# Sketched attention and a token-mixing block on one core: wider quads for batches 2 and 3, a shorter last chunk, and another written-down order

## The chip, the core and the metric

The kernel runs on one core of a Trainium2 chip. The core has five engines that each work through an instruction list of their own: TensorE (PE, whose weight loads are listed as PEld), VectorE (DVE), ScalarE (ACT), GpSimd (POOL) and SyncE (SP, which only issues DMAs here). The metric is device microseconds of one execution, as a median of several runs.

## The reference

Attention with a sketched kernel comes first (4 batches, 4 heads, 1088 tokens, head width 32; S1 and S2 are 8 x 32), and then a token-mixing block on its output x, which has 128 channels per token (4 heads of 32):

```python
phi(t) = outer(S1 @ t, S2 @ t)            # 64 features of a token and head
kv  = einsum('bhsf,bhsd->bhfd', phi(k), v)
den = einsum('bhsf,bhf->bhs', phi(q), phi(k).sum(s)) + 1e-6
x   = einsum('bhsf,bhfd->bhsd', phi(q), kv) / den      # then (b, s, h*d)
theta  = x @ w_theta
zr, zi = x * cos(theta), x * sin(theta)
y   = w_tok_r @ zr + w_tok_i @ zi         # w_tok: 1088 x 1088, over tokens
u   = x + y
out = u + relu(u @ w_ch)
```

q, k and v are float32. S1, S2 and the weights of the block come as 64-bit words and are brought to float32 in the kernel.

## The kernel before

**Data and tiles.** A batch's 1088 tokens stand as nine chunks of 128 (the last has 64 that count). Three chunks make a group, so there are three groups per batch. x is kept turned, channels on partitions, in a tile xT of 1152 columns. The two w_tok matrices come as 17 double rows of 1088 KB (row0 to row16), each loaded into a zs buffer (L642), unpacked by two ACT activations (L643, L645) and two DVE operations (L647 to L649), and kept in big buffers. The input loads of 576 KB are at L655 to L671, those of the second halves of k's chains at L714 with an accumulating DMA that POOL issues (L393). q of batch 3 arrives in 16 small DMAs (L663), since it is loaded already turned in blocks.

**Stages of a batch.** key_sums (L677), kfeatures (L767, features of k and the products with v, stage kv), chain and chain_out (L835, L933, which scale these sums), query_scale and query_slices (L985, L1007), levels (L1033: features of q as a product with weights of 128 tokens and a denominator, then lv on ACT, L1056), outputs_x (L1088: numerators, stage num), theta and z (L1169 to L1227: the products with w_theta, sine and cosine on ACT, z on DVE), and the mixing. Batches 0 and 1 are mixed by mix_row (L1256): 17 double rows of w_tok against z, summed in PSUM, and mix_out. Batches 2 and 3 are mixed together in winograd (L1352): seven block products m1 to m7 (stages named m) in place of eight, on sums of blocks of w_tok. Two of the four sums, "ac3" and "ac4" (L379, names APOOL at L153), are 16 adds of 128x544 on POOL; the other two, ac1 and ac2, are 16 such adds on DVE; zc1 to zc4 are sums of z on DVE. finish (L1282) and finish_turned (L1329, the last 160 tokens) compute u + relu(u @ w_ch) and store it.

**Numerators of batches 2 and 3.** For each group, DVE makes the features qp (L1100), turns blocks of 32 x 32 of them into qt (L1109), and TensorE runs 32 products with 32x32 weight tiles (heads of kv in bd) on 96 columns each (L1112 to L1117, the quads). Four ACT copies per group (L1121) put the results into xT. So there are three quads operations of 32 products per batch.

**Order and buffers.** Nothing is scheduled at run time. Every operation is recorded with an engine letter (P, V, A, G or S), the buffers that it reads and writes, and a number. ORDER (L34) is the sequence in which the operations are issued, written out by hand or by a planner beforehand: 1020 numbers. Each engine gets its own operations in that order. STARTS (L80) holds a planned start for each, from which two things follow. In run (L248) an operation's buffers take the free slot of their class that has been free longest. In issue (L267) padding is put before TensorE's operations between two marks (first at L431, last at L1470), `int((o.start - last - 0.08) * FILL)` products of 384 columns on an idle tile (L427, L428). This makes 28 padding products. Buffer classes (L344) are fixed numbers of slots: big 22, zs 5 of 2176 floats, g3 5 of 768 floats, g1 6, ps 8 banks of PSUM, and others. An operation whose slot still belongs to another buffer waits for that buffer's last reader.

Input loads in SP's order, before: k3, q0, row1, k2, w2, q2, row3, h1 (a second part of k of batch 1, added to the first by POOL's DMA), v0, row8, q1, row2, v1, row0, v3, h3, row7, row5, row4, h2, half of q3, row6, v2, row9, the other half of q3, row10, 13, 11, 15, 14, 12, 16. k0 and k1 are issued by ACT.

## Time and profile before

| | |
|---|---|
| time, median of 3 runs | 217.79 us (217.53 to 218.53) |
| the profiled execution: span | 215.9 us, granted clock 0.995 |
| the profiled execution: span and what lies around it | about 217.8 us |
| TensorE busy | 208.9 us, 2396 records |
| DVE, ACT, POOL busy | 174.3, 114.5, 59.7 us |
| quads (32x32 tiles, 96 columns) | 384 records |
| padding products of 384 columns | 28 |
| POOL adds 128x544 | 16, mean 1458 ns |
| first and last 10 us: TensorE busy | 7.7 us of 0 to 10; 22.0 of the last 26 |

How to read it: the page gives the busy time of each engine and its share of the span, then the span in 40 slices of 5.4 us with a digit of busy tenths per engine, the granted clock and the DMA rate; then the chain of waits that ended last; then groups of instructions (line, engine, operation, output and inputs by name, shape, count, busy time and mean of one, idle time before and what ended it). Busy time of pipelined products overlaps, so a product's mean is longer than the distance from one start to the next. A float32 product leaves two records.

### The profile page before, as it was taken

What the parts mean: (1) busy time and instruction counts of PE and PEld (TensorE: products, weight loads), DVE (VectorE), ACT (ScalarE), POOL (GpSimd) and SP (SyncE); (2) the same over time, 40 slices, a digit from 0 to 9 for tenths busy, and PEclk for the clock granted to TensorE, in tenths of its full rate; (3) what the DMA queues carried; (4) which work ended last, traced back from release to release, by engine and by line L of the source; (5) the groups of instructions that cost most, each with busy time, mean ns of one, the idle gap of its engine ahead of it and who ended that gap; (6) DMA issues with size and microseconds to landing.
All of it is one profiled execution on the core that took longest, in us unless ns stands there. A gap on an engine that the chain in (4) does not pass through costs nothing.

```text
span 215.9 us, 5832 instructions
## 1 busy us (share of the span) xinstructions
PE 208.9 (97%) x2396; PEld 152.8 (71%) x2396; DVE 174.3 (81%) x343; ACT 114.5 (53%) x256; POOL 59.7 (28%) x105
## 2 busy tenths in 40 slices
PE   7899999999999999999999999999999999999992
PEld 7677798868866666866668666667677776666781
DVE  1799998999999998999999798885994747456263
ACT  4899989999998895798704233363810000000000
POOL 1272740306400000604004100000006489950403
PEclk9999999999999999999999999999999999999998
DMA  6999999995998993192002402424050420010735
GB/s 222 395 418 419 384 365 420 425 315 97 360 285 267 416 432 145 75 308 45 0 0 32 74 3 112 114 109 112 2 88 15 67 39 0 0 23 8 125 55 103
DMA packets 28046, 37.09 MB, mean 172 GB/s; under 512 B 20564, under 2 KB 23044, under 8 KB 25844
## 3 DMA queue, kind: packets, MB, share of 16 engines
q1 hardware_dynamic: 22868, 31.86, 42.4%
q0 software_dynamic: 1552, 3.25, 7.2%
q10 hardware_dynamic: 3600, 1.62, 2.8%
q8 instruction: 19, 0.31, 0.6%
q14 instruction: 7, 0.06, 0.1%
HBM read 29.84 MB, written 4.00 MB: 157 GB/s over the span
## 4 chain that ended last, share of the span: by engine, by line
PE 63%; DMA 18%; ACT 14%; issue 2%; SPq 1%; DVE 1%; POOL 1%; POOLq 0%; ACTq 0%
PE ps L399 61%; DMA zs<-w_tok 13%; DMA big<-k_l 5%; ACT big L645 4%; ACT big L643 3%; ACT lv L1056 1%; PE ps L1131 1%; ACT big L1021 1%; ACT g L1199 1%; ACT g L1202 1%; ACT g L1205 1%; ACT g L1203 1%; POOL out L1299 1%; SPq L671 0%; ACT g L1135 0%
## 5 line engine op out<-in xcount | busy, mean ns | idle before, releaser
L399 PE MATMUL ps<-big,zs 128*128 128x384 f32 (+2 forms) x380 | 110.5, 436 | 0.0
L399 PEld LDWEIGHTS ps<-big,zs 128*128 128x128 f32 x380 | 66.9, 190 | 32.5
L379 POOL TENSOR_TENSOR big<-big,big 128x544 f32<-128x544 f32 x16 | 22.1, 1458 | 48.6 <-DVE big L379 44.6
L399 PE MATMUL ps<-big,big 128*32 128x32 f32 (+2 forms) x352 | 22.8, 234 | 0.0
L643 ACT ACTIVATE big<-zs 128x1088 f32<-128x1088 f32 x17 | 20.9, 1231 | 1.5 <-DMA zs<-w_tok 0.9
L379 DVE CUSTOM_DVE_ANT_0 big<-big,big 128x2176 uint16<-128x2176 uint16 x17 | 21.5, 1275 | 0.0
L645 ACT ACTIVATE big<-zs 128x1088 int32<-128x1088 uint32 (+1 forms) x18 | 21.4, 1194 | 0.3 <-DMA zs<-w_tok 0.3
L1338 ACT COPY big<-ps 80x256 f32<-80x256 f32 x1 | 0.4, 368 | 39.6 <-DMA out<-g 39.6
L399 PEld LDWEIGHTS ps<-big,big 128*32 128x32 f32 (+1 forms) x352 | 15.3, 124 | 6.8 <-issue 0.8
L1276 ACT COPY g<-ps 128x384 f32<-128x384 f32 (+1 forms) x6 | 2.5, 466 | 23.4 <-PE ps L399 23.4
L379 DVE TENSOR_TENSOR big<-big 128x544 f32<-128x544 f32 x8 | 9.5, 1204 | 5.6 <-PE ps L399 5.6
L383 DVE TENSOR_SCALAR big<-big 128x1088 int32<-128x1088 int32 x17 | 12.2, 719 | 0.0
L379 POOL TENSOR_TENSOR mf<-mv,sm 128x32 f32<-128x32 f16 (+1 forms) x3 | 0.8, 262 | 39.1 <-DVE sm L379 39.1
L428 PE MATMUL ps<-idle 128*128 128x112 bf16 (+1 forms) x67 | 10.0, 312 | 1.3 <-POOL idle L430 1.3
L379 DVE TENSOR_TENSOR g<-lv 128x768 f32<-128x768 f32 x12 | 11.1, 950 | 0.1
L399 PEld LDWEIGHTS ps<-w,big 128*128 128x128 f32 (+1 forms) x76 | 9.8, 189 | 1.4
L379 DVE TENSOR_TENSOR big<-big,hf 128x1152 f32<-128x1152 f32 x8 | 10.7, 1351 | 0.0
L399 PE MATMUL ps<-w,big 128*128 128x128 f32 (+1 forms) x76 | 10.5, 278 | 0.0
L399 PE MATMUL ps<-sbk,g 128*128 128x64 f32 x72 | 10.0, 276 | 0.3 <-ACT g L793 0.3
L379 DVE TENSOR_TENSOR zs<-zs,g 128x384 f32<-128x384 f32 (+2 forms) x24 | 9.8, 447 | 0.2
L386 DVE SCALAR_TENSOR_TENSOR big<-ps,even,big 128x384 f32<-128x384 f32 (+1 forms) x10 | 4.8, 493 | 6.3 <-PE ps L399 6.2
L1199 ACT ACTIVATE g<-ps 128x384 f32<-128x384 f32 x12 | 5.9, 504 | 7.3 <-PE ps L399 7.3
(199 smaller groups left out, 379.2 us busy)
## 6 DMA issues: line engine op xcount, KB each, us to landing
zs<-w_tok SPq DMA_DIRECT2D x17, 1088.0 KB, 10.6
big<-k_l SPq DMA_DIRECT2D x5, 576.0 KB, 13.2
big<-v_l SPq DMA_DIRECT2D x4, 576.0 KB, 15.6
big<-q_l SPq DMA_DIRECT2D x3, 576.0 KB, 10.7
big<-hf POOLq DMA_DIRECT2D x3, 576.0 KB, 10.0
far<-zs SPq DMA_DIRECT2D x3, 576.0 KB, 2.8
zs<-far SPq DMA_DIRECT2D x12, 144.0 KB, 4.3
big<-k_l ACTq DMA_DIRECT2D x2, 576.0 KB, 4.4
```

Of the source, the lines that this page charges most:

```text
L379: eng.tensor_tensor(out=o, in0=a, in1=b, op=f)
L383: (eng or V).tensor_scalar(out=o, in0=a, scalar1=s1, scalar2=s2, op0=op0, **kw)
L386: (eng or V).scalar_tensor_tensor(out=o, in0=a, scalar=s, in1=b, op0=op0, op1=op1)
L399: T.matmul(o, lhs, rhs, start=start, stop=stop, skip_group_check=True)
L428: T.matmul(nowhere()[:, :n], idle()[:, 0:P], idle()[:, :n], start=True, stop=True, skip_group_check=True)
L643: op("A", 0.22 + n * 0.0009, lambda: A.activation(dfn(), words_of(raw(), n)[1].bitcast(F32), AF.Prelu, scale=2.0**-112, alpha=-(2.0**32)), ...
L645: op("A", 0.22 + n * 0.0009, lambda: A.activation(stp(), words_of(raw(), n)[0].bitcast(U32), AF.Copy, scale=2.0**-29), [stp], [raw])
L1021: op("A", act(GW) + 0.1, lambda g=g, tr=tr: A.activation(f()[:, g * GW:(g + 1) * GW], tr(), AF.Copy, scale=s()[:, 0:1]), [(f, g)], [tr, (s ...
L1056: op("A", act(480), lambda g=g, lp=lp: A.copy(lv().rearrange("p l (c n) -> p l c n", n=HR)[:, :, g * GC:(g + 1) * GC], lp().rearrange("p c ...
L1131: T.transpose(tr()[:, i * P:(i + 1) * P], qp()[:, i * H + 2 * n:i * H + 2 * n + 2].rearrange("p h i j -> p (h i j)"), ident())
L1199: op("A", act(GW), lambda cs=cs, th=th: A.activation(cs()[:, 0], th(), AF.Copy, bias=ROUND), [(cs, 0)], [th])
L1276: op("A", act(w), lambda: A.copy(u(), yp()[:, :w]), [uT], [yp])
```

## The change

- **Quads.** The turned features of all three groups of a batch go into one buffer qt of class zs, and the 32 products of a batch are issued once, on 288 columns. Four copies of 288 columns replace twelve of 96. The DVE transposes stay three per batch.
- **Levels.** The ninth chunk uses 64 tokens as weights instead of 128 and writes 64 output rows.
- **finish_turned.** The transposes, the ACT copy and the products become operations of their own. The result is computed in a buffer of its own, yb, in place of xT, and an empty operation goes.
- **Classes.** zs becomes 2304 floats wide, g3 has 4 slots.
- **The order.** ORDER has 1001 numbers, and is another one. STARTS and the slot search go: slots are listed in SLOTS (391 buffers), and padding in GAPS, five products in three places.

What moves, in the order: kv2 to the first half (behind 45 us of TensorE's own work, before 69); kv3 to behind about 82 us; the rows of batch 0's mixing begin only after the first theta product of batch 1, and run mixed with those of batch 1; the sums of w_tok that POOL makes stand all behind ac2_0, while ac1_6, ac2_2 to ac2_7, zc3 and zc4 stand behind on DVE. SP's load order after is h1, k2, q0, k3, v0, h3, q1, h2, row1, q2, v1, w2, row0, row8, row3, half of q3, row6, row4, row5, v2, the rest of q3, row2, v3, the batch 1 round trip, row9, 7, 11, 10, 14, 13, 15, 12, 16.

The diff, cut to its core (ORDER, STARTS and SLOTS are lists of numbers):

```diff
 ORDER = (
...
-STARTS = (
...
+GAPS = {11: 1, 110: 3, 177: 1}
+SLOTS = (
...
 WARM = 0
-FILL = 5.0
...
-TILE16, TILE32, TILE64, QUAD = 0.045, 0.12, 0.15, 0.65
+TILE16, TILE32, TILE64, QUAD = 0.045, 0.12, 0.15, 1.25
...
+        for b, slot in zip([b for b in self.bufs if b.cls is not None], SLOTS):
+            b.slot = slot
+
+    def issue(self, pools, fill):
         for o in self.order:
...
+            for _ in range(GAPS.get(o.i, 0)):
+                fill()
...
-        "zs": (5, 2176),
+        "zs": (5, 2304),
...
-        "g3": (5, 768),
+        "g3": (4, 768),
...
-                    x = f()[:, (g * GC + i) * P:(g * GC + i + 1) * P]
-                    mm(o(i)[:, 2 * HR:], x, mf[b]().rearrange("p t h r -> p (t h r)"), False, i == GC - 1)
+                    c = g * GC + i
+                    n = min(P, S - c * P)
+                    x = f()[:, c * P:c * P + n]
+                    mm(o(i)[:n, 2 * HR:], x, mf[b]().rearrange("p t h r -> p (t h r)"), False, i == GC - 1)
...
+        qt = buf("zs", (NC, H, 2, SQ), F32, "qt") if b in QUADS else None
...
-                qt = buf("g3", (GC, H, 2, SQ), F32, "qt")
-                xq = [buf("ps", (GC, SQ), F32, "xq") for _ in range(NQ)]
...
+                vop(CH * R * R, lambda g=g, qp=qp: V.transpose(
+                    out=qt()[:, g * GC:(g + 1) * GC].rearrange("p c h f t -> p (c h f t)"),
+                    in_=qp().rearrange("p n i j -> p (n i j)")), [(qt, g)], [qp])
                 continue
...
+        if b in QUADS:
+            at("num", b)
+            xq = [buf("ps", (NC, SQ), F32, "xq") for _ in range(NQ)]
+
+            def quads():
+                for f in range(2):
+                    for j in range(NQ):
+                        for h in range(H):
+                            u = slice(j * SQ, (j + 1) * SQ)
+                            mm(xq[j]()[h * D:(h + 1) * D], bd()[u, f, h], qt()[u, :, h, f], f == 0, f == 1)
+
+            op("P", QUAD, quads, xq, [bd, qt], hold=[xt])
...
-            A.copy(y(), pu()[:n, 0:2 * DM])
...
+        op("P", 0.2, turned, [pu], keys, hold=[yb])
+        op("A", act(2 * DM), lambda: A.copy(y(), pu()[:n, 0:2 * DM]), [yb], [pu])
+        op("P", 0.35, products, [po], keys + [w2])
```

## The prediction

> **What bounds the kernel now.** I read the busy times first, then the slices, then the chain that ended last, then the groups and the waits of TensorE, and the timeline where DVE and POOL meet. The page's busy times:

> ```profile
> PE 208.9 (97%) x2396; PEld 152.8 (71%) x2396; DVE 174.3 (81%) x343; ACT 114.5 (53%) x256; POOL 59.7 (28%) x105
> ```

> TensorE is busy in all but 7 us. Its slices and the DMA's tell that there are two stages:

> ```profile
> PE   7899999999999999999999999999999999999992
> ...
> ACT  4899989999998895798704233363810000000000
> POOL 1272740306400000604004100000006489950403
> ...
> GB/s 222 395 418 419 384 365 420 425 315 97 360 285 267 416 432 145 75 308 45 0 0 32 74 3 112 114 109 112 2 88 15 67 39 0 0 23 8 125 55 103
> ```

> A slice is 5.4 us. Up to about 48 us the loads move some 400 GB/s, ACT and DVE are full, and TensorE's busy time there is partly padding. From 50 us to the end TensorE runs product after product. The chain of waits agrees:

> ```profile
> PE 63%; DMA 18%; ACT 14%; issue 2%; SPq 1%; DVE 1%; POOL 1%; POOLq 0%; ACTq 0%
> PE ps L399 61%; DMA zs<-w_tok 13%; DMA big<-k_l 5%; ACT big L645 4%; ACT big L643 3%; ACT lv L1056 1%; PE ps L1131 1%; ACT big L1021 1%; ACT g L1199 1%; ACT g L1202 1%; ACT g L1205 1%; ACT g L1203 1%; POOL out L1299 1%; SPq L671 0%; ACT g L1135 0%
> ```

> In order of time this chain is loads of k and w_tok to 31.6 us, ACT unpacking until 66, one load until 77, and TensorE from 78.4 to 210.4. So a product less after 50 us is time saved, while before 46 us what counts is when loads and unpacked rows arrive. From starts of consecutive records I get pitches (a 384-column f32 product, two records, 2 x 323 ns; a record of 128 or 96 columns about 110 ns). Adding these up in written order, TensorE's work ends at 202.65 us; its last product ends at 212.05. The difference, 9.4 us, I call the lag. It is already about 10 us at 46 us: TensorE loses time only early, and it does so to these:

> ```profile
> L399 PE MATMUL ps<-g,g 32*32 32x96 f32 x384 | 5.8, 252 | 0.0
> L428 PE MATMUL ps<-idle 128*128 128x384 bf16 x28 | 6.2, 327 | 0.0
> ```

> The first row is the quads (the numerators of batches 2 and 3), the second the 28 padding products, which stand in written order and cost their pitch of 0.163 us each, 4.6 us in all, whether the wait they were meant to fill is there or not.

> The profiled execution took its span, 215.9 us, and about 1.9 us around it, 217.8, which is the median of 217.79; terms are taken from that.

> **The quads.** Six groups of 64 records each, 384 in the row. In one group the first record starts at 119.08 us and the next 128x128 product at 119.98: 0.89 us, of which 0.72 is 64 starts and 0.17 the way back. All six: 5.34 us. After, each batch has one set: 64 records of 288 columns over 16 tiles, four per tile. A 384-column record takes 323 ns, so one of 288 takes 0.242 and four 0.97; with 0.17 behind and about 0.1 to get going, 1.25 us, an estimate. Two batches 2.50; saved 2.84. Bounds: if nothing is paid to get going, 1.13 each (saved 3.1); if starts scale with columns, 3 x 0.72 + 0.17 = 2.33 each (saved 0.7). I take 2.8, since 11 ns per record before is far under a 96-column pass (81 ns over 16 tiles is 5), so the records were bound by their starting, not by their columns. [...] The 24 ACT copies at L1121 (median 248 ns, 5.95 us) become 8 of 288 columns, some 0.39 each between that row and the 466 ns of a 384-column one (L1276): ACT wins 2.8 us, but it waits 10.0 us for TensorE at this line, so nothing on the path. The six DVE transposes (976 ns) stay. What is new is that the first copy waits for the whole batch; theta2 comes behind it, and TensorE has rows of w_tok in between, so I count nothing; without that cover it is one DVE transpose and copy, 1.4 us.

> **Levels.** The ninth chunk is 64 tokens: 8 of the 72 records of the 128x96 row (L399, mf,big) load 64 weight columns. At a pitch of 110 ns set by the weight load, up to 30 ns each go, 0.25 us in all. The nearest row with 64 weight columns (128*64, g,sm) has 0.20 to 0.26 us at each change of tile shape; if all eight changes were paid, plus 2 us. I take 0.

> **finish_turned and the buffers.** The tail's transposes, copy, products and DVE operation keep their order (transposes 211.31, copy 211.77, stores 212.7): 0. One g3 buffer less, one zs buffer longer: the new holders of these slots stand, in the engines' own sums, 10 us or more behind the last readers of the old: 0; without that cover, one product's wait of about 1 us.

> **The written order, early.** 28 padding products become 5: 23 x 0.163 = 3.75 us that are not issued. In the new order less ACT and DVE work stands in front of TensorE: by sums of the groups' means, the producers of a product were up to 2.6 us (ACT) and 1.6 us (DVE) ahead of TensorE's own sum between 16 and 44 us of its work, and are 2.4 us and more behind it now. So producers would no longer bind there. What is late next is a load. kv2 stands behind 45.2 us of TensorE's work and needs v2. In SP's new order 13 loads of 576 KB (1.51 us of sixteen engines each), seven rows of w_tok (2.83), three accumulating loads (2.25), w2 (0.67) and one or two halves of q3 (1.8) come no later than v2: 48.6 to 50.4, and about 2.2 before the first byte, so v2 lands near 51 to 53 us. SP's q3 issues held the queue from 37.1 to 51.6 us, each waiting for the eighth transfer ahead, so the queue has no slack to do better. The lag at kv2 is then about 7.3 to 8.6 us with the landing's own latency: 0.8 to 2.1 less than 9.4. I take 1.0. Bounds: minus 5 (padding and producers both gone, the loads on time) and plus 2 (row2, now behind q3 and v2, or row6 late for the unpacking, with no padding to blame).

> Sum: 217.8 - 2.8 - 0 - 1.0 = **214.0 us**. A chance of 0.42 for the forecast, 212 to 215.7.

> **Rival 1, slower: DVE kept out by POOL.** This is what the trace shows at 177 us:

> ```profile
> 175.66 5.47 POOL L379 TENSOR_TENSOR big<-big,big 128x544 f32<-128x544 f32 x4
> 177.13 4.59 DVE L379 TENSOR_TENSOR big<-big 128x544 f32<-128x544 f32 x1 [2.70 <-PE ps L399]
> ```

> A DVE add of 0.72 us (the same line's other rows) took 4.59: it got through only when POOL's four adds in a row were over. [...] Before, nearly all DVE adds of the seven-product stage are over when POOL's dense run begins, and the held one had 13 us to spare. In the new order POOL's sixteen adds start right behind ac2_0, at 159.6 us of TensorE's work, with nine DVE adds still to come whose results TensorE takes within 2 to 10 us (m6_0 at 164.1, m6_1 at 167.6, m3_0 at 170.4). POOL's pitch is 1.30 us. If a run of three holds ac2_2, it ends near 167.3, 3.2 us late; the same at ac2_7 costs 3.3 more; zc4 behind a longer run up to 7. The point: whether POOL's adds follow each other without a wait while DVE's is pending. Two holds give 214.0 + 6.5 = **220.5**. Against it: POOL waits for sums of its own (m6_0), which opens gaps, and a DVE add at 172.08 to 173.4 ran its 0.67 undisturbed when it was first, with POOL's taking 1.74. Chance 0.26.

> **Rival 2: loads do not bind.** Then padding and producers both give: 217.8 - 2.8 - 5 = **210.0**. For it: the load sums assume that all 16 engines share equally. Chance 0.12.

> **Rival 3: the early stage gives nothing or loses up to 2 us** by row2's or row6's late landing: 217.8 - 2.8 + 0 to 2 = 215.0 to 217, say **216**. Chance 0.12.

> **Rival 4: the change doesn't do what it says:** the quads' cost follows columns three to one, 0.7 saved, 1.0 early: **216.1**. Chance 0.08.

> **Numbers.** Two results of this kernel can be told apart from about 0.5%, 1.1 us: faster is below 216.7. Forecast and rival 2 are all faster; rivals 3 and 4 two thirds; 0.42 + 0.12 + 0.13 = 0.67. Same 0.08, half from the upper ends of 3 and 4 and half from one short hold. Slower 0.25, rival 1. The range from 210.0 to 220.5 leaves out about one in ten at the top and half of rival 2 at the bottom.

> **What would show it.** Quads: the row 32x288 with 128 records, 1.25 us from a set's first record to the next 128x128 product; 2.3 would be rival 4. Early: 5 padding records and kv2's first product before 53.5 us; starting at 52 or later only because v2 lands then is the forecast, at 50 rival 2. Late: DVE adds big<-big of 128x544 that take over 2 us between 165 and 185 us, and TensorE idle times released by DVE or POOL behind them, are rival 1; the forecast is wrong if these sum to over 2 us.

## The result and the profile after

The changed kernel took 245.3 us (median of four, 242.07 to 253.69) beside 217.66 for the kernel before: a ratio of 1.111, 95% interval 1.105 to 1.117. The longest two of the four, at a granted clock of 0.92 and 0.89, are left out of the ratio, which rests on 242.07 and 242.84. The profiled execution took 242.07 us, with a span of 240.1 us, 24.2 more than before, at a mean granted clock of 0.935 in place of 0.995.

The slices of the changed kernel's page (6.0 us each) show where to look:

```profile
PE 222.8 (93%) x2118; PEld 160.0 (67%) x2118; DVE 183.2 (76%) x343; ACT 116.1 (48%) x241; POOL 61.7 (26%) x105
...
PE   7998998999999999999999999999989799299990
...
DVE  1973475789699989999999998989299968914352
...
POOL 1543453006301230000000010003203699920012
PEclk9965558999999999999999999999999999859999
```

PE's digits stay at 8 and 9 in the load stage although fewer records run. The row to read is PEclk: 5 from 14 to 38 us, and a dip after 204. And one PE digit is 2, near 206 us. The chain of waits moved from loads and ACT to TensorE and DVE:

```profile
PE 70%; DVE 15%; DMA 5%; issue 4%; ACT 2%; POOL 1%; SPq 1%; POOLq 0%; DVEq 0%
```

The same stretches of the two kernels, as busy time of each engine (columns: length, PE, PEld, DVE, ACT, POOL, clock, DMA share, GB/s); the kernel before:

```profile
14.00:38.00 24.00, 23.58 (x465) 19.54 (x464) 22.93 (x50) 22.54 (x59) 9.17 (x28) 1.00 1.03 402
38.00:80.00 42.00, 41.70 (x744) 31.27 (x743) 41.44 (x74) 39.64 (x78) 8.00 (x17) 1.00 0.94 321
165.00:204.00 39.00, 39.00 (x162) 26.80 (x161) 20.62 (x37) 0.48 (x1) 25.49 (x23) 1.00 0.22 36
```

and the changed kernel:

```profile
14.00:38.00 24.00, 23.38 (x421) 20.33 (x424) 13.07 (x36) 12.28 (x40) 12.79 (x41) 0.50 1.04 364
38.00:80.00 42.00, 40.43 (x757) 31.37 (x758) 34.82 (x80) 34.90 (x86) 9.31 (x18) 1.00 0.49 159
165.00:204.00 39.00, 36.52 (x154) 24.82 (x153) 30.70 (x54) 5.77 (x13) 21.12 (x18) 1.00 0.31 64
204.00:216.00 12.00, 6.72 (x15) 3.62 (x14) 6.89 (x2) 0.00 (x0) 7.32 (x7) 0.72 0.20 32
```

From 14 to 38 us TensorE is as full as before, but at half the clock, and now DVE and ACT stand idle for 11 and 12 us, most of it waiting for TensorE (7.6 and 10.7 us), while TensorE's only wait is one of 0.6 us for nothing that the profile shows ("issue"). Adding up pitches as in the prediction, TensorE's useful work is 58.6 us at 75 us of time before and 45.4 after. That is 13.2 us lost by then, an estimate; between there and 165 us little more is lost. Padding took 4.5 us less of it, so the other losses rose by 17.7.

Late, the waits of the changed kernel's TensorE, and the DVE operation behind the longest, beside POOL's run:

```profile
PE ps L332 <- DVE zs L312: 5.3, 1, 5.3
PE ps L332 <- DVE big L312: 2.3, 2, 1.3
```

```profile
202.71 7.84 DVE L312 TENSOR_TENSOR zs<-zs 128x384 f32<-128x384 f32 x1
```

```profile
201.07 9.06 POOL L312 TENSOR_TENSOR big<-big,big 128x544 f32<-128x544 f32 x7
```

This sum of zc3 took 7.84 us (one of its shape took 0.55 at 175.5) and ended at 210.56, 0.4 us after POOL's seven adds in a row. TensorE stood for 5.3 us, and the clock was halved from 208.7 to 215.5.

### The profile page after: what moved, and what is told of

Its sections match the earlier page's. It is cut to its first block, busy times and chain, and to the rows that moved or that the text cites. A ratio compares the mean times of both kernels' runs of the same rounds, so it can differ in the third digit from the quotient of the medians.

```text
span 240.1 us, 5272 instructions
## 1 busy us (share of the span) xinstructions
PE 222.8 (93%) x2118; PEld 160.0 (67%) x2118; DVE 183.2 (76%) x343; ACT 116.1 (48%) x241; POOL 61.7 (26%) x105
## 4 chain that ended last, share of the span: by engine, by line
PE 70%; DVE 15%; DMA 5%; issue 4%; ACT 2%; POOL 1%; SPq 1%; POOLq 0%; DVEq 0%
PE ps L332 65%; DVE zs L312 4%; DVE big L312 3%; DVE g L312 2%; DMA zs<-far 2%; PE ps L951 2%; PE ps L723 2%; DMA big<-k_l 2%; DMA far<-zs 1%; PE ps L1053 1%; DVE g L319 1%; DVE sm L312 1%; DVE g L1240 1%; POOL sbk L312 1%; SPq L1102 1%
## 5 line engine op out<-in xcount | busy, mean ns | idle before, releaser
L332 PEld LDWEIGHTS ps<-big,zs 128*128 128x128 f32 x380 | 68.2, 194 | 42.6 <-POOL big L312 5.9
L332 PE MATMUL ps<-big,big 128*32 128x32 f32 (+2 forms) x352 | 24.2, 251 | 2.8 <-DVE big L312 2.3
L326 POOL DMA_DIRECT2D g<-big x6 | 5.3, 982 | 77.1 <-ACT g L1213 77.1
L332 PEld LDWEIGHTS ps<-big,big 128*32 128x32 f32 (+1 forms) x352 | 16.0, 140 | 10.4 <-issue 2.3
L332 PE MATMUL ps<-sbk,g 128*128 128x64 f32 x72 | 12.9, 330 | 0.5 <-POOL sbk L312 0.5
L319 DVE SCALAR_TENSOR_TENSOR big<-ps,even,big 128x160 f32<-128x160 f32 (+1 forms) x10 | 4.9, 490 | 10.3 <-PE ps L332 10.2
L332 PEld LDWEIGHTS ps<-sbk,g 128*128 128x128 f32 x72 | 11.4, 237 | 1.2 <-POOL sbk L312 0.9
L1236 POOL DMA_DIRECT2D out<-g x8 | 5.1, 637 | 23.5 <-DVE g L1240 21.4
L332 PEld LDWEIGHTS <-hf 128*32 128x32 bf16 (+1 forms) x252 | 8.0, 100 | 4.6 <-issue 2.4
L332 PE MATMUL ps<-mf,big 128*128 128x96 f32 (+1 forms) x72 | 9.9, 279 | 0.8 <-DVE g L312 0.8
```

The lines of the kernel that those rows point to most:

```text
L319: (eng or V).scalar_tensor_tensor(out=o, in0=a, scalar=s, in1=b, op0=op0, op1=op1)
L326: op("G", 0.9, lambda: G.dma_start(dst(), src(), accum_op=ALU.add), w, r, fly=fly)
L332: T.matmul(o, lhs, rhs, start=start, stop=stop, skip_group_check=True)
L1236: E.dma_start(out[b, s0:s0 + n, f * SQ:(f + 1) * SQ].rearrange("(c j) i -> j c i", j=SQ), ot()[f * SQ:(f + 1) * SQ, :n].rearrange("j (c i) ...
```

## The experiments

Theory 1 at first: the early loss is the half clock, which the padding kept away, and the late loss is DVE kept out by POOL. The rival for each is the order's own waits.

**Padding taken out of the kernel before.**

```diff
-FILL = 5.0
+FILL = 0.0
```

> The kernel before without its 28 padding products, all else the same. Theory 1 (the padding holds the granted clock: without it TensorE does too little per microsecond in the load stage and is granted half the clock): clock digits of 5 somewhere between 5 and 45 us, and a time 5 to 20 us above the 217.7 of before. Theory 2 (the new order and its loads cost the time, the clock only follows): clock stays at 9, and the time is within 2 us of before or up to 4 us faster.

Measured 231.56 us, 1.061 (1.058 to 1.064) of before. Its clock row:

```profile
PEclk9855555799999999799999999999999999999999
```

Beside 218.62 us for the kernel before in the same session, the padding, which takes 4.6 us of TensorE's time, is worth 12.9 us. Theory 1 holds in the old order.

**Padding put into the changed kernel**, 23 more products in GAPS, one in each 0.9 us of work:

```diff
-GAPS = {11: 1, 110: 3, 177: 1}
+GAPS = {60: 1, 104: 1, 128: 1, 68: 1, 98: 1, 150: 1, 245: 1, 26: 1, 193: 1, 155: 1, 327: 1, 134: 1, 211: 1,
+        159: 1, 107: 1, 164: 1, 436: 1, 440: 1, 220: 1, 241: 1, 125: 1, 203: 1, 224: 1, 11: 1, 110: 3, 177: 1}
```

> The changed kernel with 23 more padding products, so 28 as before, spread over 7 to 31 us of TensorE's own work, one in each 0.9 us. Theory 1: the granted clock stays at 9 up to 200 us and about 13 us of the 27 come back, 229 to 233 us. Theory 2: the 23 products add up to 3.7 us or nothing, 242 to 250.

244.03 us, 1.120 (1.113 to 1.127): nothing came back. The half clock now lasts from 22.2 to 39.3 us only, but it begins while TensorE waits 1.8 us, from 20.9 on, for nothing that the profile shows ("issue"; the expectations below read it as a wait for TensorE's own instructions, which no run shows).

**Sums moved ahead of POOL's run** (five numbers of ORDER: 930 and 931 behind 831 and 832, and 966 to 968 behind 861):

> The changed kernel with five DVE sums (zc3 of its second and third part, all zc4) moved in the written order from behind POOL's run of adds to ahead of it. Theory 1 (the late 8 us are DVE held out by POOL and the half clock that follows): no DVE operation of 8 us near 203 us, no TensorE idle time over 2 us there, no low clock digit after 200 us; 6 to 9 us less than the changed kernel, 233 to 238. Rival (TensorE waits there for the chain of sums itself, whoever makes them): 241 to 247, with the idle time at another product.

238.07 us, 1.088 (1.083 to 1.094). The 7.84 us operation is gone, and so is the idle time at 204. But three sums now stand in front of ac2, which POOL holds as well (four adds of 128x544 took 4.64 us, beside 2.62 in the run without POOL's sums below), and TensorE waits at another place:

```profile
PE ps L331 <- DVE big L311: 3.6, 2, 2.5
```

So theory and rival were both partly right: the hold moved with the order. This order also shows a second effect of POOL's run: a later product waited 1.0 us for POOL's last add itself.

**Both edits.**

> The changed kernel with both edits: 28 padding products and the five sums ahead of POOL's run. If the two causes are separate and complete, 13 + 8 us come back: 219 to 225 us, and the clock digit is 9 throughout. If the order itself loses time, over 227.

241.18 us, 1.104 (1.101 to 1.107): the late part as in the run before, and 3.1 us more than there with the 23 products of padding: they cost and gave nothing back.

**52 padding products**, and the five sums placed ahead of the sum that waits for m1 (861 and 966 to 968 before 792):

> The changed kernel with 52 padding products (one in each 0.4 us of TensorE's own work from 7 to 31 us, two more at five products around the place where TensorE waited 1.8 us for its own instructions), and the five DVE sums ahead of the sum that waits for m1. [...] Rival (the order's own waits hold TensorE back, the clock only follows): the padding only adds, 238 to 248 us.

239.59 us, 1.101 (1.093 to 1.108), with the clock full until 69 us. By theory 1 in its simple form that would have given 217 to 226 us; it falls here. The clock row and the stretches of this kernel:

```profile
PEclk9999999999988999999999999999999999999997
```

```profile
14.00:38.00 24.00, 21.54 (x514) 16.34 (x513) 15.52 (x38) 13.84 (x43) 13.45 (x42) 1.00 1.04 373
38.00:80.00 42.00, 40.68 (x723) 31.79 (x721) 31.49 (x76) 33.15 (x81) 8.13 (x16) 0.96 0.49 156
```

DVE and ACT still have a fifth of the time or more to spare, so TensorE is the bound at full clock as well. Its useful work at 75 us is 44.8 us, no more than in the changed kernel. Padding, the warm-up included, took 15.4 us by then (10.0 in the kernel before, 5.5 in the changed one). TensorE also waited 3.4 us in three places for nothing that the profile shows, two of them here:

```profile
PE ps L331 <- issue: 2.8, 2, 1.8
```

**The wide quads alone in the kernel before:**

```diff
-        "zs": (5, 2176),
+        "zs": (5, 2304),
-        "sm": (13, 192),
+        "sm": (11, 192),
+        qt = buf("zs", (NC, H, 2, SQ), F32, "qt") if b in QUADS else None
...
+            op("P", QUAD, quads, xq, [bd, qt], hold=[xt])
```

> The kernel before with the wide quads alone: one set of 32 products of 288 columns per batch, four copies of 288 columns, qt in a zs buffer (2304 wide; the class sm has 11 slots in place of 13 to make room, and three operations of theta that need the whole batch's copies move behind them). The rest, order and padding, stays. By the records of the changed kernel a set costs 1.53 us from its first record to the next product, so 2 x 1.53 in place of 6 x 0.89, 2.3 us less: 215 to 216 us. If the whole-batch wait costs a TensorE wait, up to 218.

219.1 us, 1.004 (1.000 to 1.008). TensorE waits for the last turning of features, as the timeline shows, and half the clock follows for 3.4 us:

```profile
134.60 1.93 PE L381 MATMUL ps<-zs,g 32*32 32x288 f32 x49 [2.65 <-DVE zs L1090]
```

**The same with batch 3's set later** (operation 750 behind 660, and what needs it):

> The kernel before with the wide quads alone, as in the run before this, but the set of batch 3 and what needs its copies stand five mixing products (about 2.9 us) later in TensorE's list, so that DVE's last turning of features is done when the set comes up. Theory (the wide quads save 2.3 us by themselves, and the run before this lost them to TensorE's 2.65 us wait for DVE and the 3.4 us of half clock behind it): no wait at that place, clock 9 throughout, 215 to 216 us. Rival (the whole-batch wait moves on to theta and the mixing): 217.5 to 219.

217.62 us, 0.995 (0.992 to 0.999): faster than both kernels, by less than half of what was expected and by under 1%. The half clock is gone and TensorE's work is 2.2 us less (189.4 in place of 191.6), but two new waits of 1.2 and 1.0 us take back more than half of it; the measured gain is 0.9 us:

```profile
PE ps L381 <- ACT big L1128: 1.2, 1, 1.2
...
PE ps L381 <- DVE g L368: 1.0, 1, 1.0
```

The first is the copies of the whole batch, the wait that I had costed at nothing.

**33 padding products, five more at the place of the 1.8 us.**

> The changed kernel with 33 padding products (the 28 of the earlier run and five more at the two products where TensorE waited 1.8 us for its own instructions), and the five DVE sums early. If the half clock is what the load stage costs: digit 9 from 5 to 45 us and 229 to 234 us, 8 us less than with 28. If the stage of the new order takes its time whatever the clock (as 52 padding products with a full clock gave 239.6): 237 to 242.

242.3 us, 1.107 (1.099 to 1.115). The wait without a releaser came again (1.8 us at 20.9), and the half clock was 13.7 us long, 24.6 to 38.2. The padding took what the clock gave.

**The changed kernel without POOL's sums:**

```diff
-                op(e, pool_(HT) if e == "G" else dve(HT), lambda i=i: tt(E, dst[0](i), x[0](i), y[0](i), f), [dst[1](i)],
+                op(e, pool_(HT) if e == "G" else dve(HT), (lambda: None) if e == "G" else lambda i=i: tt(E, dst[0](i), x[0](i), y[0](i), f), [dst[1](i)],
```

> The changed kernel without POOL's 16 adds of 128x544 (the sums ac3 and ac4 are left out, so the products m3, m7 and m4 run on other data); all else the same. Theory (the late loss is DVE held out by POOL): no DVE add over 1.5 us after 165 us, no TensorE idle time over 1 us there but the one near 173 us, no low clock digit behind 200 us, and 8 to 10 us less than the changed kernel in the same session, 232 to 236. Rival (DVE's own chain is late): the idle time near 204 us stays, 240 to 245.

231.23 us, 1.055 (1.048 to 1.063); the profiled span is 229.0, 11.1 less than the changed kernel's. TensorE's only wait over 0.8 us behind the start is the one near 173 us:

```profile
PE ps L332 <- DVE big L312: 1.0, 1, 1.0
```

and the clock row has no dip behind 38 us:

```profile
PEclk9975556999999999999999999999999999999997
```

The late loss is POOL's run of adds, with the half clock behind it. Record by record, 0.9 of the 11.1 us had arisen by 30 us, where the edit does nothing, so the late loss is 10.3. This run does not separate DVE being held out from TensorE's own waits for POOL's sums, since both are gone. In the run with the sums early a product waited for POOL's last add; in the changed kernel that add ended at 210.13, some 2 us after TensorE would have come to the same product had zc3 been there. So about 2 of the 10.3 us would have stayed without the hold, an estimate. What is left, 231, is near what the old order takes without padding (231.56), but that is no sign of one cause: half the clock lasted 34 us there and 24 here.

**30 padding products in front, and 41.**

> The changed kernel with 30 padding products, all but one in front of the products that ran until 30 us in the run with 52, and the five DVE sums early. Theory A (half clock costs what padding would; the new order has a long stretch of small tiles and needs both): TensorE's work at 45 us is no further than with 5, 33 or 52 padding products, and the time is 237 to 242 us. Theory B (52 were enough but too many): digit 9 until 45 us, 229 to 234 us.

> The same with 41 padding products, eleven more, on the chain and rest products between 25 and 34 us of the run with 52. Theory A: 237 to 242 us whatever the clock digit. Theory B: digit 9 until 45 us, and 3 to 6 us less than the run with 52, 233 to 237 us.

239.66 us, 1.096 (1.089 to 1.103), and 241.15, 1.105 (1.100 to 1.109): within theory A's numbers. Theory B was not put to the test, because neither profiled execution kept the clock to 45 us; with 30 products the row is

```profile
PEclk9999995555899999999999999999999999999999
```

Both profiled executions (245.91 and 250.18 us) were also the longest of their four; the other three of each had a mean clock of 0.96 to 0.98. In both profiles, the long waits without a releaser stand behind the same numbers of records, whatever operation comes next: behind 348 (0.6 us) and behind 600 (4.1 and 2.4). The 4.1 us, from 32.6 to 36.7, are where the clock fell.

**11 padding products in the kernel before** (FILL 2.5).

> The kernel before with 11 padding products in place of 28 (the factor FILL halved). [...] If the clock follows the mean over the stage: digit 9, 217 to 219 us.

Ten executions of this one program took 217.9 to 228.6 us (median 223.7), and the clock tells them apart: 0.99 or 1.00 in the four up to 218.6, 0.94 to 0.96 in the six from 223.6. The profiled one, 228.56 us, has two windows of 3.41 us (the step in which the granted clock changed, see the last section) with low work, 0.31 and 0.28 of what the array could stream, and this clock row:

```profile
PEclk9769555699999999999999999999999999999999
```

So 11 products are at the edge: one program, with one sum of work in its load stage, gave both results, 5 to 10 us apart. That single windows decide, and that only their place differs between the executions, is argued: of those at full clock there is no trace.

## Why the prediction was wrong, point by point

- **Quads.** Mechanism right, size near. A set takes 1.53 us from its first record to the next product, not 1.25: two sets 3.06 in place of 5.34, 2.3 us saved of the 2.84 forecast and inside its bounds. The 64 starts took 1.20 of it and the way back 0.33, where 0.97, 0.17 and 0.1 had been added up. The prediction lists the quads under time that is lost early, but they run from 119 us on. "Nothing" for the copies' wait held in the new order; in the old order it cost 1.2 us. One of the two sets, and what follows it:

```profile
142.60 1.60 PE L332 MATMUL ps<-zs,g 32*32 32x288 f32 x64
144.13 3.17 PE L332 MATMUL ps<-big,zs 128*128 128x320 f32 x10
```

- **Levels.** Taken as 0; the 8 records with 64 weight columns begin 0.20 us after the last of 128 and 0.18 ahead of what follows, where 0.11 was usual. With 0.13 between the two that is 0.18 us a batch, 0.7 us more in all.
- **finish_turned.** 0 for its own steps, nearly right: from the transposes to its last store's issue 1.5 us before, 1.7 after. But in the new order other stores end last, behind a DVE transpose that ends at 235.7. From TensorE's last product to the end of the span it is 5.4 us in every trace of the new order and 3.7 in every one of the old, so the tail cost 1.7 us that the prediction had at nothing. The stores:

```profile
236.02 1.22 POOL L1236 DMA_DIRECT2D out<-g  x2 [1.57 <-DVE g L1240]
```

- **The padding, and with it the early term.** This is the step that failed: "cost their pitch of 0.163 us each, 4.6 us in all, whether the wait they were meant to fill is there or not". From it came the early term, 1.0 us less, with bounds of 5 less and 2 more; about 13 more were measured. The padding's cost was right; that it brings nothing was not looked at. In the old order it kept the clock: 12.9 us are lost without it. In the changed kernel half the clock lasted 23.9 us, which is at most 12 us lost, an estimate. But putting padding back returned none of it, so the clock alone does not account for the early loss in the new order.
- **The order's own cost to TensorE** has no term in the sum. I count the places where consecutive products, padding left out, stand on tiles of another shape (rows x weight columns): 105 in the changed kernel, 68 in the kernel before, and by 75 us 87 against 46. Over 1024 such places at full clock in the 14 traces the next product started 0.10 us (median) later than the pitch. Wide quads take away 8 of them and the ninth chunk's 64 weight columns add 7, so the order itself adds 38, about 4 us, an estimate; no run tests this by itself. With it the early account nearly closes: -4.5 (padding) + 12 (half clock, at most) + 1 (waits) + 4 (changes of shape) is 12.5 of the 13.2 us. With 52 padding products, at nearly full clock, 5.4 + 3.1 + 4 and 1.7 for the dip at 69 us are 14.2, where 13.8 (58.6 - 44.8) were lost.
- **What is late next.** "So producers would no longer bind there" was right (DVE and ACT idle for 11 us and more). "What is late next is a load" was wrong. v2 was issued at 49.8 us and had landed by 58.8, while kv2's features were made by DVE only at 58.2 to 60.9. kv2's first product came at 64.5 us, 19.3 behind TensorE's own sum where 7.3 to 8.6 was forecast, and TensorE did not stand waiting for it. Next was TensorE itself. In its first 30 us of useful work, by pitches, the new order has 719 records on tiles of less than half the array, the old one 531. At half the clock a product's pitch nearly doubles (64 columns on the whole array: 0.213 us in place of 0.112); at full clock, with 52 padding products, the padding (15.4 us by 75 us), changes of tile shape (about 4, the estimate above) and waits without a releaser (3.4) fill the time. The clean-pitch sum, which I used as TensorE's need, holds for neither.
- **Rival 1** was right in mechanism and place, and its point decided as stated: POOL's adds followed each other, five and seven in a row. Its price was too small: 6.5 us for two holds, where POOL's run cost 10.3. It also fell elsewhere: the holds of ac2, which the 6.5 stood for, cost TensorE 1.3 us, and 5.3 came with zc3, which the prediction didn't name (zc4 it did, "up to 7", outside the sum). It came at 188 to 210 us, not at 165 to 185. The half clock behind the 5 us wait was left out; 4.8 us of it fell on running products, about 2.4 us lost.
- **The sum.** -2.3 (quads) + 0.7 (levels) + about 13 (load stage) + 1.0 (a wait for DVE near 173 us, which stays without POOL's adds) + about 10 (late) + 1.7 (tail) is about 24, of the 24.2 us by which the span grew. The range ended at 220.5 because no case held the clock or a cost of the order itself, and because the late rival was not added to another one.

What stays open: whether the 13 us of the load stage divide as estimated above, since no run gave TensorE its full clock for nothing or the new order with fewer changes of tile shape. Padding of 28 to 52 products, in five placements, never bought it for less than it gave; that no placement does was not shown. What the waits without a releaser are for is not shown either: the traces show only that they stand at fixed record numbers, and none of them in the old order with its full padding.

## What to carry to other kernels

Read the clock row before and after as a resource of its own: a product that computes nothing may be what holds it (28 of them were worth 12.9 us in the old order), and an order is also a distribution of array work over time. Before regrouping small products early, add up how much of the array each few microseconds use, and count the changes of tile shape (0.10 us each at the median here). And where one engine's operations hold another's up, as POOL's adds did here with a DVE add (7.84 us in place of 0.55), look for long runs on the one behind which short, urgent operations of the other are queued, and add the clock that a long wait costs.
